# Cross attention and gated FFN on one core: the gate columns' load moved ahead, and the order of all engines up to the loop laid out anew

## The chip, the cores and the metric

The kernel runs on one core of a Trainium2 chip. A core has TensorE (matmuls; PE in the profile, its weight loads PEld), VectorE (DVE), ScalarE (ACT), GpSimd (POOL) and SyncE (SP), each of which works through its own instructions in order and waits on semaphores for the others, and 16 DMA engines that move data between HBM and the on-chip memory (SBUF). Matmul results go to PSUM, which has eight banks here. The metric is the device time in microseconds (us).

## The reference

Two stages. An attention between a sequence x (8 batches, 8 heads, 512 positions, 64 columns) and a small state (32 rows for each head), read in both directions with the same scores; its output is the input of a gated feed-forward network.

```
B, H, S, Ns, D = (8, 8, 512, 32, 64)
scores = scale * x @ state.T            # for each batch and head, scale = 1/8
xread  = softmax(scores) @ state        # 512 rows
sread  = softmax(scores.T) @ x          # 32 rows
t      = concatenate(xread, sread)      # 544 rows for each batch, 512 columns (8 heads of 64)
out    = (sigmoid(t @ w_gate) * (t @ w_val)) @ w_out      # 512 -> 1536 -> 512
```

Inputs and output are float32; the kernel computes its matmuls in bfloat16.

## The kernel before, in words

Since `xread` is a product with the small state, the kernel never forms it. It multiplies the state with the gate and value weights once for each batch (`sw_*`, giving SW: state rows by 1536 columns, for two groups of heads) and then multiplies SW with the transposed softmax weights aT (`gv_half`, `gv_mm`). So for each batch b there are these steps:

- `load_x`, `load_xh`, `load_xp` bring x; `cast_x`, `cast_xp` make it bfloat16. `xT_mm` transposes it on TensorE into PSUM and `xT_cp` copies that to SBUF (batches 0 and 1); from batch 2 on `at_xT_dma` transposes it with four DMAs on SP's queue, one for each quarter (chunk) c of the positions.
- `S_mm(b, i)` makes the scores: for batches 0 and 1 for half of the heads, from batch 2 on for chunks 2i and 2i + 1. `S_exp` takes the exponential, `n_sum` and `n_mul` sum and scale. `Sq_mm`, `Sq_exp`, `nq_sum`, `nq_mul` do the same for a quarter of the heads (one pair), batch 0 alone.
- The scaled weights are transposed to aT: `aT_mmc` and `aT_cp` (batches 0 and 1) or `aT_dma` (DMA transposes, later batches).
- `at_Eb`, `rd_mm` and `rd_fin` make `sread`: a bfloat16 copy of the exponentials on POOL, matmuls with x, and the division.
- `sw_half`, `sw_visit`, `sw_wide` make SW for a stretch of the weight columns; `sw_cp` copies a PSUM bank of it to SBUF, on ACT or DVE.
- `gv_half(b, f, w, place)` makes the gate (w = 0) or value (w = 1) of a block f of 128 of the 1536 columns; `gv_th` takes the tanh on ACT and `gv_glu` multiplies on DVE.
- `out_mm(b, k)` multiplies four blocks with w_out. From batch 1 on a Strassen-like scheme with sums (`t_sum`, `s_sum`) takes its place, in the loop.

The order of every engine is written out by hand: the kernel calls these helpers one after the other, and each engine gets its instructions in the order of the calls. Up to line 886 the calls are single lines (the stretch that the change lays out anew): the start, all of batch 0, the gates of batches 0 and 1, and the scores of batch 2. Then a loop (`step(b, f)`) runs over batches 2 to 8 and 12 blocks each, where batch 8 stands for the `sread` rows of all batches.

What sets the order beside the calls: each `place` is a set of PSUM banks that rotate (GV has two, SWP four, OU and AT one each), so a matmul into a bank waits for the copy out of its former content. DMAs with a cast, and some loads, are issued by POOL's queue: the weight columns (`load_w`), x of batches 0 to 3, w_out (`load_wo`, three thirds), the later state rows (`load_sb`). x of the later batches, the transposes and the stores of the output go by SP's queue. `warm` runs dummy matmuls into an unused bank.

The lines that the prediction's steps touch: L306 and L322 (SW matmuls), L385 and L373 (gate and value), L418 (`out_mm`), L154 and L163 (`S_mm`), L181 (`Sq_mm`), L285 (`rd_mm`), L147 (xT by DMA), L268 (aT by DMA), L103 and L85 (loads of x), L107 (weight columns), L114 (w_out), L551 (state rows), L593 (`pad`, which copies transposed state rows to a padded form on POOL), L233 (`n_mul`). L111 is `gate(landed)`: a copy of one column of a tile on POOL, so that POOL's queue holds until that tile has landed; in the old order it stands ahead of the load of batch 3's x and waits for batch 2's xT.

```
def gate(landed):
    nc.gpsimd.tensor_copy(pre[:, 1:2], landed)

def at_xT_dma(b):
    xT = xT_tile(b)
    for c in range(4):
        nc.sync.dma_start_transpose(xT[:, :, c], xbs[b][:, c].rearrange("p h d -> p (h d)"))
```

Of the kernel before, what the change touches and what calls it, by code (L numbers as in the profile page):

```python
# [16 lines left out]
def kernel(  # L17
# [86 lines left out]

    def load_w(w, lo, n):
        src = (moe_w_gate, moe_w_val)[w].rearrange("(k p) n -> p k n", p=128)
        nc.gpsimd.dma_start((wg, wv)[w][:, :, lo:lo + n], src[:, :, lo:lo + n])  # L107
# [533 lines left out]
    xT_mm(0, 1, GV)
    xT_cp(0, 0, vec)
    xT_cp(0, 1, vec)
    nq_sum(0, 3)
# [9 lines left out]
    xT_cp(1, 0, act, 2)
    xT_cp(1, 3, act)
    warm(2, AT)
    xT_mm(1, 2, GV)
    sw_half(0, 256, 256, 0, (OU, AT))
    nq_mul(0, 2, pool)
# [3 lines left out]
    sw_cp(0, 256, 0, 0, act)
    n_mulc(0, 0, 0, vec)
    S_mm(1, 0, SWP)
    aT_mmc(0, 1, SWP)
# [3 lines left out]
    aT_mmc(0, 0, SWP)  # L670
    at_Eb(0)
    aT_cp(0, 0, vec)
    aT_cp(0, 1, act)
    sw_half(0, 256, 256, 1, (GV, OU))
# [23 lines left out]
    sw_visit(1, 256, 256)
    gv_half(0, 9, 0, GV)
    sw_cp(0, 1024, 1, 0, vec)  # L700
    n_mul(1, 0, pool)
    sw_cp(1, 256, 2, 0, act)
    n_mul(1, 1, pool)
    sw_cp(0, 1024, 1, 1, vec)
    sw_cp(1, 256, 2, 1, act)
    load_w(0, 512, 512)
    aT_mmc(1, 1, AT)
    gv_glu(0, 3)
    at_Eb(1)
    aT_mmc(1, 0, GV)  # L710
    gv_th(0, 9)
    aT_cp(1, 0, vec)
    gv_half(0, 9, 1, OU)
    sw_visit(1, 1024, 256)
    load_sb(1)
    aT_cp(1, 1, act)
    sw_visit(0, 0, 256)
    sw_cp(0, 0, 2, 1, act)
# [24 lines left out]
    sw_cp(0, 1280, 2, 1, vec)
    load_w(1, 512, 512)
    load_x(2, nc.gpsimd)
    gv_half(0, 11, 0, GV)
    gv_th(0, 11)
    rd_fin(1)
    load_wo(0)
    sT_mm(1, SWP)  # L750
    gv_glu(1, 8)
    gv_half(0, 11, 1, AT)
    sT_cp(1, act)
    load_wo(1)
    gv_half(0, 1, 1, GV)
# [44 lines left out]
    gv_th(0, 7)  # L800
    gv_half(0, 7, 1, GV)
    sw_wide(2, 1)
    sw_cp(2, 1, 0, 1, act)
# [4 lines left out]
    out_mm(0, 0, AT)
    sw_cp(2, 1, 0, 0, vec)
    sw_visit(1, 0, 256)  # L810
    sw_cp(2, 1, 1, 0, act)
    sw_cp(2, 1, 2, 0, vec)
# [16 lines left out]
    gv_glu(1, 10)
    gv_glu(1, 6)  # L830
    out_mm(0, 4)
    out_mm(0, 11)
# [3 lines left out]
    gv_mm(1, 4, GV)
    gv_mm(1, 5, SWP)
    gv_glu(1, 1)
    t_sum(1, nc.vector)
    S_exp(2, 0)  # L840
    n_sum(2, 0)
    gv_th(1, 4)
    gv_th(1, 5)
    n_mul(2, 0, pool)
    S_mm(2, 1, AT)
    gv_glu(1, 5)
    S_exp(2, 1)
    n_sum(2, 1)
    out_mm(0, 1, GV)
    sw_wide(2, 0)  # L850
    sw_cp(2, 0, 1, 1, act)
    aT_dma(2, 0)
    n_mul(2, 1, pool)
    sw_cp(2, 0, 0, 0, act)
    at_Eb(2)
    sw_cp(2, 0, 2, 1, act)
    sw_cp(2, 0, 2, 0, vec)
    sw_cp(2, 0, 1, 0, act)
    out_mm(0, 3)
    aT_dma(2, 1)  # L860
    out_mm(0, 5)
    gv_mm(1, 7, SWP)
    gv_th(1, 7)
    gv_glu(1, 4)
    gv_mm(1, 11, GV)
    pad(4, 4)
    sw_cp(2, 0, 0, 1, vec)
    t_sum(2, nc.vector)
    t_sum(3, nc.vector)
    gv_th(1, 11)  # L870
    cast_x(3, pool, 4, 4)
    cast_x(3, act, 0, 4)
    gv_mm(1, 0, SWP)
    at_xT_dma(3)
    gv_th(1, 0)
    gv_glu(1, 11)
    out_mm(0, 6, GV)
    out_mm(0, 8)
# [202 lines left out]
```

## Time and profile before

| | before |
|---|---|
| device time, median of 3 runs | 213.7 us (213.7 to 214.9) |
| device time of the profiled execution | 214.2 us |
| its span, first to last instruction | 212.4 us |
| PE busy | 206.5 us, 97% |
| DVE busy | 162.0 us, 76% |
| ACT busy | 128.4 us, 60% |
| POOL busy | 73.0 us, 34% |
| granted clock of TensorE | 1.0 |
| moved by DMA | 27.01 MB |

The span leaves out what lies around the first and the last instruction. Matmuls are pipelined and their ends are modelled in the profile, so a busy PE is not PE at its peak, and an instruction's own duration is longer than the step from one matmul to the next. "Idle before" is the time that an engine waited ahead of an instruction, and the arrow names what ended it; a releaser is inferred from semaphores.

### The profile page before, as it was taken

What the parts mean: (1) busy time and instruction counts of PE and PEld (TensorE: products, weight loads), DVE (VectorE), ACT (ScalarE), POOL (GpSimd) and SP (SyncE); (2) the same over time, 40 slices, a digit from 0 to 9 for tenths busy, and PEclk for the clock granted to TensorE, in tenths of its full rate; (3) what the DMA queues carried; (4) which work ended last, traced back from release to release, by engine and by line L of the source; (5) the groups of instructions that cost most, each with busy time, mean ns of one, the idle gap of its engine ahead of it and who ended that gap; (6) DMA issues with size and microseconds to landing.
All of it is one profiled execution on the core that took longest, in us unless ns stands there. A gap on an engine that the chain in (4) does not pass through costs nothing.

```text
span 212.4 us, 5290 instructions
## 1 busy us (share of the span) xinstructions
PE 206.5 (97%) x2075; PEld 128.5 (60%) x2075; DVE 162.0 (76%) x315; ACT 128.4 (60%) x243; POOL 73.0 (34%) x101
## 2 busy tenths in 40 slices
PE   8899999999999999999999999999999999999992
PEld 2554433544565666565656575656666666788882
DVE  5698897784975779767986789588967787777882
ACT  3699696586778557865786478647874453233210
POOL 7899370259245404560437023902410000000000
PEclk9999999999999999999999999999999999999999
DMA  6999999685889544926911460245020400130026
GB/s 167 206 198 199 268 231 154 125 232 99 115 219 291 55 81 163 271 59 144 313 41 36 77 222 15 43 85 215 0 42 18 197 5 0 66 135 0 3 83 214
DMA packets 40152, 27.01 MB, mean 127 GB/s; under 512 B 23616, under 2 KB 37184, under 8 KB 40128
## 3 DMA queue, kind: packets, MB, share of 16 engines
q1 hardware_dynamic: 29376, 18.69, 33.8%
q0 software_dynamic: 10320, 7.67, 22.0%
q10 hardware_dynamic: 432, 0.33, 0.6%
q8 instruction: 16, 0.26, 0.5%
q14 instruction: 8, 0.07, 0.2%
HBM read 18.35 MB, written 8.91 MB: 128 GB/s over the span
## 4 chain that ended last, share of the span: by engine, by line
PE 86%; DMA 8%; ACT 2%; issue 1%; DVE 1%; SPq 0%; ACTq 0%
PE gvp L385 36%; PE outp L457 29%; DMA xf<-in_x_dram 8%; PE gvp L388 5%; PE swp L306 4%; PE outp L507 2%; PE outp L418 2%; PE swp L322 2%; PE gvp L373 1%; PE outp L476 1%; PE Sp L154 1%; PE rdp L282 1%; DVE glu L400 1%; ACT th L394 1%; PE Sp L163 0%
## 5 line engine op out<-in xcount | busy, mean ns | idle before, releaser
L394 ACT ACTIVATE th<-gvp 128x512 f32<-128x512 f32 (+1 forms) x108 | 62.1, 577 | 52.9 <-PE gvp L385 36.3
L385 PE MATMUL gvp<-aT,SW 128*128 128x512 bf16 x352 | 93.2, 379 | 0.1
L400 DVE SCALAR_TENSOR_TENSOR glu<-th,gvp 128x512 bf16<-128x512 f32 x96 | 65.1, 685 | 31.6 <-PE gvp L385 14.4
L359 ACT CAST SW<-swp 128x512 bf16<-128x512 f32 (+1 forms) x83 | 45.3, 581 | 8.0 <-PE swp L306 7.6
L385 PEld LDWEIGHTS <-SW 128*128 128x128 bf16 x352 | 32.2, 98 | 25.0 <-issue 6.2
L457 PEld LDWEIGHTS <-Sm 128*128 128x128 bf16 x324 | 31.7, 98 | 12.6
L206 POOL CAST Eb<-E 128x256 bf16<-128x256 f32 x32 | 17.5, 579 | 47.7 <-ACT E L174 47.7
L457 PE MATMUL outp<-tw,Sm 128*128 128x256 bf16 x240 | 31.8, 273 | 0.0
L457 PEld LDWEIGHTS <-glu 128*128 128x128 bf16 x240 | 23.5, 98 | 10.2
L457 PE MATMUL outp<-wo,glu 128*128 128x256 bf16 x168 | 22.9, 273 | 0.0
L233 POOL TENSOR_TENSOR ab<-E,ri 128x512 bf16<-128x512 f32 x14 | 14.6, 1050 | 19.4 <-DVE ri L216 19.2
L439 DVE TENSOR_TENSOR Sm<-glu 128x768 bf16<-128x768 bf16 (+1 forms) x27 | 15.3, 569 | 0.0
L465 DVE SCALAR_TENSOR_TENSOR res<-outp,U 128x512 f32<-128x512 f32 x19 | 13.0, 684 | 0.0
L388 PE MATMUL gvp<-XS,wgv 128*128 128x256 bf16 x96 | 12.6, 273 | 0.0
L174 ACT ACTIVATE E<-Sp 128x512 f32<-128x512 f32 x15 | 9.0, 603 | 4.9 <-PE Sp L154 3.8
L123 POOL CAST xb<-xf 128x1024 bf16<-128x1024 f32 x11 | 11.1, 1038 | 1.5 <-DMA xf<-in_x_dram 1.5
L406 DVE SCALAR_TENSOR_TENSOR glu<-th,gvp 128x128 bf16<-128x128 f32 x24 | 8.7, 462 | 3.8 <-PE gvp L388 3.7
L359 DVE CAST SW<-swp 128x512 bf16<-128x512 f32 (+1 forms) x17 | 10.1, 623 | 1.9 <-PE swp L322 1.7
L418 PE MATMUL outp<-wo,glu 128*128 128x512 bf16 x48 | 11.5, 379 | 0.0
L457 PE MATMUL outp<-wo,Sm 128*128 128x256 bf16 x84 | 11.5, 273 | 0.0
L214 DVE TENSOR_REDUCE rs<-E 128x16 f32<-128x512 f32 x15 | 10.2, 677 | 0.8 <-ACT E L174 0.8
L271 POOL CAST xs<-xf 128x1024 bf16<-128x1024 f32 x10 | 10.2, 1043 | 0.0
(105 smaller groups left out, 204.8 us busy)
## 6 DMA issues: line engine op xcount, KB each, us to landing
out_dram<-res SPq DMA_DIRECT2D x13, 512.0 KB, 2.9
xf<-in_x_dram SPq DMA_DIRECT2D x4, 1024.0 KB, 7.6
xf<-in_x_dram POOLq DMA_DIRECT2D x2, 1024.0 KB, 9.8
out_dram<-res SPq DMA_DIRECT2D x7, 256.0 KB, 3.0
wo<-in_moe_w_out_dram POOLq DMA_DIRECT2D x3, 512.0 KB, 10.6
wgv<-in_moe_w_gate_dram POOLq DMA_DIRECT2D x4, 256.0 KB, 7.6
wgv<-in_moe_w_val_dram POOLq DMA_DIRECT2D x4, 256.0 KB, 8.1
xf<-in_x_dram SPq DMA_DIRECT2D x3, 256.0 KB, 3.8
```

What stands on the lines that cost most here:

```text
L123: cp(xbs[b].rearrange("p c h d -> p h c d")[:, lo:lo + n], (xhs if b in xhs else xfs)[b][:, lo:lo + n])
L206: nc.gpsimd.tensor_copy(Ebs[b][:, c], E1s[b][:, c])
L233: (nc.gpsimd if eng is pool else nc.vector).tensor_tensor(half(b, i, abs_), e1, ri.unsqueeze(len(ri.shape)).to_broadcast(e1.shape), ALU.mult)
L359: cp(*sw_left.pop((b, lo, w, e)))
L385: nc.tensor.matmul(ps, SWs[b][:, g, w, fs], aTs[b][:, :, g], start=(g == 0), stop=(g == 1))
L388: nc.tensor.matmul(ps, (wg, wv)[w][:, j, fs], XS[:, :, j], start=(j == 0), stop=(j == 3))
L394: nc.scalar.activation(th, held["gv", b, f][0], AF.Tanh, scale=0.5)
L400: nc.vector.scalar_tensor_tensor(glus[b][:, f], held["th", b, f], 1.0, held["gv", b, f][1], ALU.add, ALU.mult)
L418: nc.tensor.matmul(ops[b, c], glus[b][:, f, c * 128:(c + 1) * 128], wo[:, f], start=(f == 0), stop=(f == NF - 1))
L439: nc.vector.tensor_tensor(Sm[:, t, i], a, c, op)
L457: nc.tensor.matmul(wps[key][:, c], lhs[:, i, c * 128:(c + 1) * 128], rhs[:, i], start=(first and c == 0 and i == 0), stop=(i == NF // 2 - ...
L465: nc.vector.scalar_tensor_tensor(to, wps[key], 0.5, held["w", name], ALU.mult, ALU.add)
```

## The change

The helper functions stay as they are; the list of calls up to the loop is another. The number of each kind of step is the same, but for the scores of batch 0: `S_mm(0, 0)`, `S_exp(0, 0)`, `n_sum(0, 0)` and two `n_mulc` (the first half of the heads) become two quarters with `Sq_mm`, `Sq_exp`, `nq_sum` and `nq_mul`. What the prediction speaks of:

- On POOL's queue `load_w(0, 256, 256)` (gate columns 256 to 511) stands ahead of the two loads of batch 1's x, where it stood behind them.
- The gate/value halves, SW groups, copies and GLUs of batches 0 and 1 stand in another order, with some copies on the other engine; `n_mul(1, 0)` moves from POOL to DVE, `sT_cp(1)` from ACT to DVE.
- `S_mm(2, 0)` stands behind `out_mm(0, 2)`, ahead of `gv_mm(1, 10)`, `gv_mm(1, 1)`, `out_mm(0, 4)`, `out_mm(0, 11)` and `sT_mm2`.
- POOL's queue: the load of w_out's last third between the two casts of batch 2's x; the load of batch 3's x behind the second cast, and `gate` behind `at_Eb(2)`; `pad(4, 4)` ahead of both `n_mul` of batch 2.

The core of the diff:

```diff
+    load_w(0, 256, 256)
     load_xh(1, 0, 4)
-    load_xh(1, 4, 4)
     make_identity(nc, ident)
     warm(2, OU)
-    load_w(0, 256, 256)
+    load_xh(1, 4, 4)
     load_w(1, 256, 256)
...
-    S_mm(0, 0, SWP)
...
-    S_exp(0, 0)
...
-    n_sum(0, 0)
-    n_mulc(0, 0, 1, vec)
...
+    Sq_mm(0, 0, GV)
...
+    Sq_mm(0, 1, SWP)
...
+    n_mul(1, 1, pool)
...
+    n_mul(1, 0, vec)
...
-    pad(2, 2)
...
-    cast_x(2, pool, 4, 4)
...
-    cast_x(2, pool, 0, 4)
-    at_xT_dma(2)
...
-    load_wo(2)
...
+    cast_x(2, pool, 0, 4)
+    load_wo(2)
...
+    cast_x(2, pool, 4, 4)
...
+    load_x(3, nc.gpsimd)
...
+    load_sb(2)
+    pad(2, 2)
...
+    at_xT_dma(2)
...
     out_mm(0, 9)
-    gv_mm(1, 10, SWP)
-    gv_th(1, 10)
-    out_mm(0, 2)
...
+    out_mm(0, 2)
+    S_mm(2, 0, SWP)
+    S_exp(2, 0)
+    out_mm(0, 11)
+    gv_mm(1, 10, GV)
...
-    gate(xTs[2][:, 0, 3, 0:1])
-    load_x(3, nc.gpsimd)
...
-    sT_mm2(SWP)
-    S_mm(2, 0, SWP)
-    sT_cp2(act)
...
+    sT_mm2(SWP)
+    S_mm(2, 1, OU)
...
+    pad(4, 4)
...
+    n_mul(2, 0, pool)
...
+    cast_x(3, pool, 4, 4)
...
+    at_Eb(2)
     gate(xTs[2][:, 0, 3, 0:1])
...
     at_xT_dma(3)
```

More of the change, by code (lines that the diff above doesn't have):

```diff
@@ L641 @@
[L641 to L644, printed above, removed]
+    xT_mm(0, 3, SWP)
+    warm(1, AT)
+    xT_mm(0, 0, GV)
+    sT_pad(1, act)
+    xT_cp(0, 3, vec)
+    Sq_mm(0, 3, SWP)
+    xT_cp(0, 0, act)
+    Sq_exp(0, 3)
+    xT_mm(0, 2, OU)
+    cast_xp(0, act, 2, 2)
+    Sq_mm(0, 0, GV)
+    xT_cp(0, 2, vec)
+    Sq_exp(0, 0)
+    warm(1, AT)
+    Sq_mm(0, 2, AT)
+    nq_sum(0, 3)
+    Sq_exp(0, 2)
+    xT_mm(0, 1, SWP)
+    xT_cp(0, 1, act)
+    warm(1, GV)
+    nq_sum(0, 0)
@@ L645 @@
+    sw_half(0, 256, 256, 0, (GV, OU))
+    warm(2, AT)
+    Sq_mm(0, 1, SWP)
+    xT_mm(1, 0, OU, 2)
     warm(2, AT)
-    S_mm(0, 0, SWP)
-    xT_mm(1, 0, GV, 2)
-    Sq_exp(0, 2)
-    nq_mul(0, 3, pool)
+    warm(1, AT)
+    sw_cp(0, 256, 0, 1, act)
     nq_sum(0, 2)
-    warm(1, AT)
-    xT_mm(1, 3, GV)
-    S_exp(0, 0)
[L654 to L659, printed above, removed]
-    n_sum(0, 0)
-    n_mulc(0, 0, 1, vec)
+    sw_cp(0, 256, 0, 0, act)
@@ L662 @@
+    Sq_exp(0, 1)
+    xT_cp(1, 0, act, 2)
+    nq_mul(0, 3, vec)
+    nq_mul(0, 0, pool)
+    nq_mul(0, 2, pool)
+    xT_mm(1, 2, SWP)
+    nq_sum(0, 1)
+    xT_mm(1, 3, GV)
+    S_mm(1, 0, OU)
+    nq_mul(0, 1, vec)
+    xT_cp(1, 3, vec)
+    aT_mmc(0, 1, SWP)
+    aT_mmc(0, 0, AT)
     xT_cp(1, 2, act)
[L663 to L666, printed above, removed]
     S_exp(1, 0)
+    at_Eb(0)
+    aT_cp(0, 1, act)
+    aT_cp(0, 0, vec)
     S_mm(1, 1, SWP)
-    sw_cp(0, 256, 0, 1, vec)
@@ L670 @@
[L670 to L674, printed above, removed]
+    load_sb(1)
+    load_w(0, 1280, 256)
     S_exp(1, 1)
-    rd_mm(0, GV)
+    sw_half(0, 256, 256, 1, (SWP, GV))
+    rd_mm(0, SWP)
+    n_sum(1, 0)
     sw_cp(0, 256, 1, 0, act)
-    gv_half(0, 3, 0, AT)
     sw_cp(0, 256, 1, 1, act)
-    gv_half(0, 2, 0, SWP)
-    n_sum(1, 0)
+    rd_fin(0)
+    gv_half(0, 2, 0, GV)
+    gv_half(0, 3, 0, OU)
+    gv_half(0, 2, 1, AT)
     sw_half(0, 1024, 256, 0, (SWP, SWP))
+    sw_visit(1, 256, 256)
@@ L698 @@
[L698 to L718, printed above, removed]
@@ L740 @@
-    gv_half(1, 3, 0, SWP)
-    gv_th(0, 1)
-    gv_th(1, 3)
[L743 to L755, printed above, removed]
-    pad(2, 2)
-    gv_half(0, 10, 0, GV)
+    sw_cp(0, 1024, 0, 1, act)
+    sw_cp(0, 1024, 1, 1, act)
+    n_mul(1, 0, vec)
+    gv_half(0, 8, 0, SWP)
+    sw_cp(0, 1024, 1, 0, vec)
@@ new lines @@
+    gv_glu(0, 2)
+    gv_glu(0, 3)
+    sw_cp(1, 256, 2, 1, vec)
+    gv_half(0, 9, 0, SWP)
+    aT_mmc(1, 1, SWP)
+    sw_cp(1, 256, 2, 0, act)
+    gv_th(0, 8)
+    aT_cp(1, 1, vec)
+    aT_mmc(1, 0, AT)
+    aT_cp(1, 0, vec)
+    gv_half(0, 9, 1, GV)
+    gv_th(0, 9)
+    gv_half(0, 8, 1, OU)
+    sw_visit(1, 1024, 256)
+    gv_glu(0, 9)
+    gv_glu(0, 8)
+    sw_visit(0, 0, 256)
+    load_w(0, 512, 512)
+    at_Eb(1)
+    sw_cp(1, 1024, 2, 0, act)
+    gv_half(1, 2, 0, GV)
+    rd_mm(1, AT)
@@ new lines @@
+    sw_cp(1, 1024, 2, 1, act)
+    gv_half(1, 8, 0, GV)
+    load_w(1, 512, 512)
+    gv_half(1, 2, 1, OU)
+    sw_cp(0, 0, 2, 0, vec)
+    gv_half(1, 8, 1, GV)
+    gv_th(1, 2)
+    sw_cp(0, 0, 2, 1, act)
+    gv_half(0, 1, 0, SWP)
+    gv_th(1, 8)
+    rd_fin(1)
+    sw_visit(0, 1280, 256)
+    gv_half(0, 1, 1, GV)
+    gv_half(1, 3, 0, SWP)
+    sT_mm(1, GV)
+    gv_half(0, 0, 0, SWP)
+    gv_glu(1, 2)
+    gv_glu(1, 8)
+    sw_cp(0, 1280, 2, 1, vec)
+    sw_cp(0, 1280, 2, 0, vec)
+    gv_half(0, 0, 1, SWP)
@@ L758 @@
+    load_x(2, nc.gpsimd)
+    load_sb(3)
+    gv_th(0, 1)
+    load_wo(0)
+    gv_half(0, 11, 0, AT)
+    sT_cp(1, vec)
+    load_wo(1)
+    gv_th(0, 0)
+    nc.scalar.activation(pre[:, 0:1], ones, AF.Exp)
+    gv_half(0, 11, 1, SWP)
+    gv_half(0, 10, 0, OU)
+    gv_half(1, 9, 0, GV)
+    gv_glu(0, 1)
+    cast_x(2, pool, 0, 4)
+    load_wo(2)
+    gv_half(1, 3, 1, GV)
+    gv_th(0, 11)
+    gv_glu(0, 0)
+    gv_th(1, 3)
+    gv_glu(0, 11)
+    gv_th(1, 9)
+    gv_th(0, 10)
     sw_visit(0, 512, 512, 0)
-    gv_glu(0, 0)
@@ L793 @@
-    gv_half(0, 7, 0, GV)
-    sw_cp(1, 512, 0, 0, act)
+    gv_half(0, 6, 1, GV)
+    gv_th(0, 4)
     gv_half(0, 5, 1, SWP)
+    gv_half(0, 7, 0, SWP)
+    load_x(3, nc.gpsimd)
     sw_cp(1, 512, 0, 1, act)
     sw_cp(1, 512, 1, 1, act)
+    sw_cp(1, 512, 1, 0, act)
+    sw_cp(1, 512, 0, 0, vec)
+    load_sb(2)
+    pad(2, 2)
+    gv_half(0, 7, 1, GV)
+    gv_glu(0, 4)
+    gv_th(0, 7)
+    sw_wide(2, 1)
+    gv_mm(1, 6, GV)
+    sw_cp(2, 1, 0, 0, act)
+    sw_cp(2, 1, 0, 1, act)
+    out_mm(0, 7, OU)
@@ L798 @@
+    out_mm(0, 0, AT)
     gv_glu(0, 6)
     gv_glu(0, 5)
[L800 to L803, printed above, removed]
+    at_xT_dma(2)
     gv_glu(0, 7)
-    gv_mm(1, 6, GV)
+    sw_cp(2, 1, 1, 0, vec)
+    sw_cp(2, 1, 2, 0, act)
     sw_cp(2, 1, 2, 1, act)
+    sw_visit(1, 0, 256)
+    sw_visit(1, 1280, 256)
     sw_cp(2, 1, 1, 1, act)
[L808 to L812, printed above, removed]
@@ L813 @@
-    sw_visit(1, 1280, 256)
-    out_mm(0, 7, OU)
-    gv_th(1, 6)
-    out_mm(0, 9)
-    sw_cp(1, 1280, 2, 0, act)
-    sw_cp(1, 1280, 2, 1, vec)
-    gv_mm(1, 10, SWP)
+    sw_cp(1, 0, 2, 0, act)
+    gv_th(1, 6)
+    sw_cp(1, 1280, 2, 1, act)
+    sw_cp(1, 1280, 2, 0, vec)
+    sw_cp(1, 0, 2, 1, vec)
+    t_sum(0, nc.vector)
+    gv_glu(1, 6)
+    out_mm(0, 9)
+    out_mm(0, 2)
[3 more added lines that the diff above has]
+    gv_mm(1, 10, GV)
+    n_sum(2, 0)
+    gv_mm(1, 4, SWP)
@@ L820 @@
     gv_th(1, 10)
-    out_mm(0, 2)
-    sw_cp(1, 0, 2, 1, vec)
-    sw_cp(1, 0, 2, 0, vec)
-    t_sum(0, nc.vector)
     gv_mm(1, 1, SWP)
+    gv_glu(1, 10)
+    t_sum(1, nc.vector)
+    gv_th(1, 4)
+    gv_mm(1, 5, GV)
     gv_th(1, 1)
-    gate(xTs[2][:, 0, 3, 0:1])
-    load_x(3, nc.gpsimd)
[L829 to L832, printed above, removed]
-    sT_mm2(SWP)
-    S_mm(2, 0, SWP)
-    sT_cp2(act)
[L836 to L873, printed above, removed]
+    sT_mm2(SWP)
+    S_mm(2, 1, OU)
+    t_sum(2, nc.vector)
+    gv_th(1, 5)
+    sT_cp2(act)
+    S_exp(2, 1)
+    pad(4, 4)
+    t_sum(3, nc.vector)
+    gv_glu(1, 1)
+    n_mul(2, 0, pool)
+    out_mm(0, 4)
+    out_mm(0, 1, GV)
+    out_mm(0, 3)
+    gv_glu(1, 5)
+    gv_glu(1, 4)
+    sw_wide(2, 0)
@@ new lines @@
+    aT_dma(2, 0)
+    n_sum(2, 1)
+    n_mul(2, 1, pool)
+    sw_cp(2, 0, 1, 0, act)
+    sw_cp(2, 0, 0, 1, act)
+    sw_cp(2, 0, 0, 0, act)
+    cast_x(3, pool, 4, 4)
+    out_mm(0, 5)
+    aT_dma(2, 1)
+    gv_mm(1, 7, SWP)
+    gv_mm(1, 11, GV)
+    gv_mm(1, 0, SWP)
+    out_mm(0, 6, GV)
+    sw_cp(2, 0, 2, 0, act)
+    gv_th(1, 11)
+    gv_th(1, 7)
+    out_mm(0, 8)
+    sw_cp(2, 0, 1, 1, vec)
+    cast_x(3, act, 0, 4)
+    gv_th(1, 0)
+    sw_cp(2, 0, 2, 1, vec)
+    at_Eb(2)
+    gate(xTs[2][:, 0, 3, 0:1])
@@ L874 @@
+    gv_glu(1, 11)
     at_xT_dma(3)
[L875 to L878, printed above, removed]
     out_mm(0, 10)
```

85 lines of the change are left out of this document (18 added, 67 removed).

## The prediction

> **What bounds the kernel now.** I read the page first, then busy time by stretches, then the chain of waits, then single engines around the places where the order changes.
>
> ```profile
> span 212.4 us, 5290 instructions
> ...
> PE 86%; DMA 8%; ACT 2%; issue 1%; DVE 1%; SPq 0%; ACTq 0%
> ```
> ```profile
> 4.50:13.40 8.90, 8.02 (x145) 5.32 (x145) 6.17 (x17) 6.38 (x13) 7.86 (x13) 1.00 1.41 207
> 13.40:32.05 18.65, 18.65 (x207) 7.71 (x204) 16.59 (x33) 15.69 (x33) 13.87 (x21) 1.00 1.31 228
> 32.05:41.78 9.73, 9.73 (x93) 4.40 (x93) 7.18 (x12) 5.56 (x11) 1.09 (x2) 1.00 1.09 139
> 41.78:54.65 12.87, 12.73 (x155) 5.84 (x151) 9.12 (x17) 9.47 (x19) 9.15 (x11) 1.00 0.65 164
> 54.65:185.00 130.35, 130.20 (x1263) 83.68 (x1257) 101.16 (x180) 83.22 (x154) 37.64 (x46) 1.00 0.43 108
> ```
>
> The columns after the length are busy us of PE, PEld, DVE, ACT and POOL, then the granted clock. From 13.40 on TensorE is busy in every stretch, at full clock, up to the tail. Its work is the same after the change: the same matmuls (eight of the 64-column score matmuls change their line) and 17 warm-up matmuls in both. So the end can move in three ways only: TensorE starts its dense work earlier than 13.4, an existing wait goes, or a new one comes. An edit that merely reorders work under a full TensorE is worth nothing.
>
> One wait stands where the profile's chain leaves TensorE, at the hand-over to the loop:
>
> ```profile
> 40.87 10.51 DMA xf<-in_x_dram
> ...
> 52.97 1.30 DVE glu L400 x2
> ...
> 54.31 0.41 PE swp L322 x7
> ```
> ```profile
> 44.94 0.63 PE L306 MATMUL swp<-wgv,sTc 64*32 64x512 bf16 x16
> ...
> 45.71 1.47 PE L418 MATMUL outp<-wo,glu 128*128 128x512 bf16 x6
> ```
> ```profile
> 53.35 0.63 PE L306 MATMUL swp<-wgv,sTc 64*32 64x512 bf16 x16
> ...
> 54.65 0.61 PE L385 MATMUL gvp<-aT,SW 128*128 128x512 bf16 x2
> ```
>
> The load of batch 3's x holds ACT's cast, the cast holds the tanh behind it, that holds the GLU on DVE, and the GLU holds the PSUM bank of the 24-matmul SW group. The undisturbed group occupies 45.71 - 44.94 = 0.77 us, this one 54.65 - 53.35 = 1.30 us: TensorE waits 0.53 us.
>
> **The change, part by part.** *The start.* The first gate columns trade places with batch 1's x, and batch 0's scores come in quarters, so its chain (exp, sum, scale, transpose) ends earlier.
>
> ```profile
> 5.00 0.78 POOL L107 DMA_DIRECT2D wgv<-in_moe_w_val_dram  x1
> ```
> ```profile
> wgv<-in_moe_w_val_dram POOLq DMA_DIRECT2D x1, 256.0 KB, 7.5
> ```
> ```profile
> 12.62 0.30 PE L306 MATMUL swp<-wgv,tw 64*32 64x256 bf16 x8
> ...
> 13.43 0.38 PE L385 MATMUL gvp<-aT,SW 128*128 128x512 bf16 x1
> ```
>
> The first value columns land at 5.00 + 7.5 = 12.5, and the SW half that needs them starts at 12.62. In the new order the same five transfers stand up to them on POOL's queue, so 12.5 stays; and this SW half and `rd_mm(0)` still stand ahead of the first gate matmul, so that cannot come before 12.5 + (13.43 - 12.62) = 13.3, against 13.43. The set of work done by then is the same. The gain is 0 to 0.1; I take 0. Against it, the second half of batch 1's x now lands one transfer later, and its transposes, copies and `S_mm(1, 1)` must pass before that SW half: up to 0.4 us lost. That would be hidden by the wait found below, which ends at a DMA and not at TensorE's own pace; alone it would cost its 0.4.
>
> *From 13.4 to 32.* Up to `sw_wide(2, 1)` the same set of gate/value halves and SW groups is permuted. ACT has 18.65 - 15.69 = 3.0 us free there and DVE 2.1. DVE takes over one `n_mul` and one `sT_cp` and gives two SW copies to ACT, roughly an exchange. POOL loses the `n_mul`, which brings forward only the issues behind it. I take 0, between a loss of 0.5 and none. No gain is possible, since TensorE shows no idle time there. The cover is the full TensorE; if a wait of a few tenths appears, it too shortens the wait below.
>
> *The scores of batch 2.* `S_mm(2, 0)` stands in the old order behind two `gv_mm`, three `out_mm` and `sT_mm2` counted from 37.00; in the new order only `out_mm(0, 2)` is left between.
>
> ```profile
> 37.00 1.03 PE L373 MATMUL gvp<-aT,SW 128*128 128x512 bf16 x4
> 37.87 1.03 PE L418 MATMUL outp<-wo,glu 128*128 128x512 bf16 x4
> ...
> 41.78 0.40 PE L154 MATMUL Sp<-sTz,xT 128*128 128x64 bf16 x8
> ```
>
> One such group lasts 37.87 - 37.00 = 0.87 us, so TensorE reaches `S_mm(2, 0)` at 37.00 + 0.87 = 37.87 and no more at 41.78. The scores read xT of batch 2, chunk 0 and, four matmuls on, chunk 1. These come by DMA transposes on SP's queue.
>
> ```profile
> 19.92 0.93 POOL L85 DMA_DIRECT2D xf<-in_x_dram  x1
> 20.81 1.53 POOL L114 DMA_DIRECT2D wo<-in_moe_w_out_dram  x2
> ...
> 29.20 2.02 POOL L123 CAST xb<-xf 128x1024 bf16<-128x1024 f32 x2 [1.19 <-DMA xf<-in_x_dram]
> 31.17 0.75 POOL L114 DMA_DIRECT2D wo<-in_moe_w_out_dram  x1
> 40.34 0.19 POOL L111 CAST pre<-xT 128x1 f32<-128x1 bf16 x1 [8.43 <-DMA xT<-xb]
> 40.87 0.91 POOL L85 DMA_DIRECT2D xf<-in_x_dram  x1 [0.34 <-PE outp L418]
> ```
> ```profile
> 31.25 6.38 SPq L147 DMA_TRANSPOSE xT<-xb  x4
> ...
> 45.45 7.33 SPq L268 DMA_TRANSPOSE aT<-ab  x4
> ```
> ```profile
> xf<-in_x_dram POOLq DMA_DIRECT2D x1, 1024.0 KB, 9.2
> ...
> wo<-in_moe_w_out_dram POOLq DMA_DIRECT2D x1, 512.0 KB, 12.4
> ...
> wo<-in_moe_w_out_dram POOLq DMA_DIRECT2D x1, 512.0 KB, 7.5
> ...
> xT<-xb SPq DMA_TRANSPOSE x1, 7.7
> ...
> xT<-xb SPq DMA_TRANSPOSE x1, 6.7
> ...
> xf<-in_x_dram POOLq DMA_DIRECT2D x1, 1024.0 KB, 10.5
> ...
> aT<-ab SPq DMA_TRANSPOSE x1, 6.1
> ```
> ```profile
> L147 SPq DMA_TRANSPOSE xT<-xb x4: 1217/1260/1273, 72.5 to 76.3; - x4
> ...
> DMA to landing us min/median/max: 2.5/2.5/2.5
> ```
>
> The numbers at the ends are us from issue to landing, each of one DMA: the load of batch 2's x (issued 19.92), the second and third third of w_out (the second issued half of 1.53 behind 20.81, the third at 31.17), the first two transposes of xT (31.25, and one issue of 1.3 later, 32.6), batch 3's x (40.87), the first transpose of aT (45.45). On free DMA engines, in the loop, a transpose lands 2.5 after its issue. Beside a load it takes 6 to 8, and it ends just behind that load: w_out's third lands at 31.17 + 7.5 = 38.7, the transposes at 31.25 + 7.7 = 38.95 and 32.6 + 6.7 = 39.3; batch 3's x lands at 40.87 + 10.5 = 51.4, the transpose of aT at 45.45 + 6.1 = 51.55. Old TensorE arrived at 41.78, after 39.3, and never saw this; the old gate at 40.34 kept batch 3's x out of these transposes' way.
>
> The change puts both together. On POOL the third load of w_out now stands between the two casts: casts at 29.2 and 30.95, transposes issued from 31.95 on, 0.7 later than before. Right behind the second cast, at 31.95 as well, POOL issues batch 3's x; the gate, moved behind `at_Eb(2)`, holds nothing any more. So a load of a megabyte is in flight beside the transposes, behind w_out's third.
>
> When does it land? Batch 2's x lands at 29.1 and w_out's second third at 21.6 + 12.4 = 34.0: 2.4 us each for two loads with as many bytes to read as batch 3's x. At that pace w_out's third lands at 36.4 and batch 3's x at 38.8: the lower end. The upper end is its own 10.5 from issue, 42.4. The nearest row is w_out's third, which beside the transposes and two small state loads took 38.7 - 34.0 = 4.7 and not 2.4, so I take a value in the upper half, 41.0. Chunk 1 landed 39.3 - 38.7 = 0.6 behind its load: 41.6, between 39.4 and 43.0. TensorE is ready at 37.87 and stands still for 3.7 us (1.5 to 5.1). Every engine's queue goes on behind that, and TensorE has no slack later to win it back.
>
> [...]
>
> *The hand-over.* Batch 3's x lands some 10 us before its casts are due, so the 0.53 us at 54.31 goes: next late there is the aT of batch 2. Its scaling on POOL now stands behind `pad(4, 4)`, a new wait for the state transposes (`sT_mm2`, ACT's copies); behind it queue both `n_mul`, the cast of batch 3 and Eb.
>
> ```profile
> 44.38 1.04 POOL L233 TENSOR_TENSOR ab<-E,ri 128x512 bf16<-128x512 f32 x1 [2.61 <-DVE ri L216]
> ...
> 49.87 1.28 POOL L593 COPY sTz<-sTc 64x512 bf16<-64x512 bf16 x2
> ```
>
> With `S_mm(2, 0)` ending at 41.9, five groups of 0.87 and `sT_mm2` (as long as half a group) bring 46.7, copies a similar half 47.2, the pad 48.5, two `n_mul` of 1.04 50.6; four transposes 1.3 apart with one store between leave SP by 54.5 and land 2.5 later, 57.0. The loop needs them at 54.65 + 3.2 = 57.85. The margin of 0.8 is thin but enough: cost 0.
>
> **The sum.** 3.7 - 0.5 = +3.2 us, from +1.0 (1.5 - 0.5) to +4.6. The profiled execution took 214.2 (span 212.4 and 1.8 around it) and would take 217.4; it lies 0.5 above the median of the runs, 213.7, so the forecast is 213.7 + 3.2 = **216.9**.
>
> **Rivals.** *Held back no more than before* (0.24): the transposes suffer from w_out's third alone. Chunk 1 lands at the old 39.3, or 6.7 after its new issue at 33.3, 40.0: wait 1.4 to 2.1, time 214.6 to 215.3. For it: batch 3's x queues behind w_out's third. Against it: aT ended behind batch 3's x itself.
>
> *The transposes get their turns* (0.10): chunk 1 lands 2.5 after 33.3, at 35.8, before 37.87. Then nothing waits, the 0.53 is won, and the time is 213.2, not slower. It decides at one point: chunk 1 landed by 37.87. For it stands the loop's 2.5; against it three transposes in the rows above. [...]
>
> *Faster by over 1%* (0.04): TensorE would have to be dense 2 us before 13.4, against the value columns' 12.5; so perhaps the columns land earlier than their place says.
>
> *The aT of batch 2 comes late as well* (0.07): one of its transposes behind stores takes 6.1 instead of 2.5, landing at 60.6, 2.8 past its due time: 219.7.
>
> **How the numbers follow.** The main case has 0.55 and covers 215.6 to 218.4. Over 1% is 2.1 us, beyond 215.8 or below 211.6; the three runs shown spread over 0.6%, so less would hardly be told from none. Slower: 0.55 less a sliver of 0.02 near its lower end, plus 0.07, 0.60. Within 1%: 0.24 + 0.10 + 0.02 = 0.36. Faster: 0.04. The range 213.0 to 218.7 holds nearly all of the main case and the first two rivals and leaves out some 0.17.
>
> **What would show it.** In the new profile: first gate matmul at 13.3 to 13.8; POOL's issue of batch 3's x near 32; TensorE idle for 2 to 5 us from about 38 before the scores of L154, with the DMA of xT as releaser; chunk 1 landing just behind batch 3's x; the SW group at the loop's head back at 0.77 us. I am wrong if L154 starts near 38 with no idle time before it, or if TensorE has its idle time somewhere before 32.

## The result and the profile after

The changed kernel takes 223.2 us (median of 5 runs, 222.1 to 223.9) against 213.7 for the kernel before: 1.043 times its time, 95% interval 1.039 to 1.047. The direction was forecast; the size, 9.5 us, is three times the 3.2 forecast and lies outside the range.

The head of the profile after and its chain by engine:

```profile
span 221.3 us, 5286 instructions
...
PE 78%; DMA 13%; POOL 3%; ACT 2%; issue 1%; SPq 1%; DVE 0%; POOLq 0%; ACTq 0%
```

TensorE holds 78% of the chain where it held 86%, and DMA 13% where it held 8%. The view by stretches (length, busy us of PE, PEld, DVE, ACT and POOL, granted clock, DMA share, GB/s) says where:

```profile
4.50:13.49 8.99, 7.89 (x147) 5.14 (x147) 5.92 (x16) 7.76 (x17) 8.54 (x14) 1.00 1.40 205
13.49:32.60 19.11, 18.52 (x206) 7.76 (x202) 16.18 (x33) 15.07 (x33) 10.57 (x16) 1.00 1.33 227
32.60:38.73 6.13, 6.08 (x60) 2.35 (x60) 3.55 (x7) 4.38 (x9) 2.69 (x5) 1.00 1.18 158
38.73:48.80 10.07, 3.37 (x16) 1.41 (x16) 2.17 (x4) 1.19 (x2) 0.00 (x0) 0.66 0.99 131
48.80:63.50 14.70, 14.60 (x165) 6.84 (x166) 9.83 (x17) 9.92 (x19) 7.76 (x12) 1.00 0.28 82
```

The start is as long as before (13.49 against 13.43). One stretch of ten microseconds, 38.73 to 48.80, has TensorE busy for 3.37 of them at two thirds of its clock. The first gate matmul of the loop comes at 63.50 and not at 54.65: 8.85 later, which is the whole difference of the two spans (8.9). TensorE in order of time there:

```profile
36.99 1.90 PE L418 MATMUL outp<-wo,glu 128*128 128x512 bf16 x8
44.87 0.39 PE L154 MATMUL Sp<-sTz,xT 128*128 128x64 bf16 x4 [5.98 <-DMA xT<-xb]
45.98 0.40 PE L154 MATMUL Sp<-sTz,xT 128*128 128x64 bf16 x4 [0.72 <-DMA xT<-xb]
46.19 1.90 PE L418 MATMUL outp<-wo,glu 128*128 128x512 bf16 x4
```

Eight output matmuls at one per 0.215 us end at 38.71; then TensorE stands until chunk 0 of xT(2) has landed, runs four score matmuls, and stands again for chunk 1. POOL's row of issues, and what each DMA took from issue to landing:

```profile
31.12 0.75 POOL L114 DMA_DIRECT2D wo<-in_moe_w_out_dram  x1
31.86 1.05 POOL L123 CAST xb<-xf 128x1024 bf16<-128x1024 f32 x1
32.85 0.91 POOL L85 DMA_DIRECT2D xf<-in_x_dram  x1
33.74 0.75 POOL L551 DMA_DIRECT2D Sm<-in_state_dram  x1
```
```profile
32.95 8.84 SPq L147 DMA_TRANSPOSE xT<-xb  x4
```
```profile
wo<-in_moe_w_out_dram POOLq DMA_DIRECT2D x1, 512.0 KB, 7.2
...
xf<-in_x_dram POOLq DMA_DIRECT2D x1, 1024.0 KB, 11.9
...
xT<-xb SPq DMA_TRANSPOSE x1, 11.9
...
Sm<-in_state_dram POOLq DMA_DIRECT2D x1, 64.0 KB, 12.2
...
xT<-xb SPq DMA_TRANSPOSE x1, 11.5
```

Batch 3's x lands at 32.85 + 11.9 = 44.75 and the first transpose at 32.95 + 11.9 = 44.85; the state rows land at 33.74 + 12.2 = 45.9 and the second transpose, issued at 34.4, at 45.9 too. The first four matmuls aside (0.2 us at this clock, 46.19 - 45.98 for the second four), TensorE stood for 6.2 + 0.9 = 7.1 us, where 3.7 were forecast.

The clock was not forecast at all. The same view cut at the granted clock:

```profile
38.73:41.97 3.24, 0.16 (x1) 0.00 (x0) 1.23 (x2) 0.00 (x0) 0.00 (x0) 1.00 1.03 233
41.97:44.87 2.90, 0.00 (x1) 0.01 (x1) 0.00 (x0) 0.00 (x0) 0.00 (x0) 0.50 1.70 115
44.87:48.80 3.93, 3.21 (x15) 1.40 (x16) 0.94 (x2) 1.19 (x2) 0.00 (x0) 0.50 0.45 60
```

The clock fell to half 3.3 us after the work ran out and stayed there for 3.93 us after it came back. The 2.8 us from 45.98 on, at half speed, cost 1.4.

The hand-over to the loop is as forecast, 63.50 - 62.73 = 0.77 us for the SW group:

```profile
62.73 0.62 PE L306 MATMUL swp<-wgv,sTc 64*32 64x512 bf16 x16
63.17 0.40 PE L322 MATMUL swp<-wgv,sTc 64*32 64x512 bf16 x8
63.50 1.04 PE L385 MATMUL gvp<-aT,SW 128*128 128x512 bf16 x4
```

So the two profiled executions add up: TensorE came to the scores at 38.71 instead of 37.87 (0.84 late), stood for 7.1, lost 1.4 to the clock and won 0.53 back: 8.8 of the 8.85.

### The profile page after: what moved, and what is told of

Its sections match the earlier page's. It is cut to its first block, busy times and chain, and to the rows that moved or that the text cites. A ratio compares the mean times of both kernels' runs of the same rounds, so it can differ in the third digit from the quotient of the medians.

```text
span 221.3 us, 5286 instructions
## 1 busy us (share of the span) xinstructions
PE 207.9 (94%) x2072; PEld 128.6 (58%) x2075; DVE 160.3 (72%) x313; ACT 130.3 (59%) x249; POOL 70.7 (32%) x100
## 4 chain that ended last, share of the span: by engine, by line
PE 78%; DMA 13%; POOL 3%; ACT 2%; issue 1%; SPq 1%; DVE 0%; POOLq 0%; ACTq 0%
PE gvp L385 28%; PE outp L457 28%; DMA xf<-in_x_dram 8%; DMA xT<-xb 5%; PE gvp L388 5%; PE outp L418 4%; PE gvp L373 3%; PE swp L306 3%; PE outp L507 2%; PE Sp L154 1%; PE outp L476 1%; PE swp L322 1%; POOL wgv L107 1%; PE rdp L282 1%; ACT th L394 1%
## 5 line engine op out<-in xcount | busy, mean ns | idle before, releaser
L359 ACT CAST SW<-swp 128x512 bf16<-128x512 f32 (+1 forms) x88 | 47.5, 578 | 11.1 <-PE swp L306 8.9
L206 POOL CAST Eb<-E 128x256 bf16<-128x256 f32 x32 | 16.0, 530 | 49.8 <-ACT E L174 49.8
L233 POOL TENSOR_TENSOR ab<-E,ri 128x512 bf16<-128x512 f32 x13 | 13.9, 1066 | 17.4 <-DVE ri L216 16.3
L174 ACT ACTIVATE E<-Sp 128x512 f32<-128x512 f32 x14 | 8.4, 602 | 12.2 <-PE Sp L154 11.7
L214 DVE TENSOR_REDUCE rs<-E 128x16 f32<-128x512 f32 x14 | 9.5, 680 | 7.1 <-ACT E L174 7.1
L418 PE MATMUL outp<-wo,glu 128*128 128x512 bf16 x45 | 11.9, 402 | 0.2
L457 PE MATMUL outp<-wo,Sm 128*128 128x256 bf16 x84 | 11.5, 273 | 0.0
L154 PE MATMUL Sp<-sTz,xT 128*128 128x64 bf16 x96 | 5.2, 197 | 6.7 <-DMA xT<-xb 6.7
L359 DVE CAST SW<-swp 128x512 bf16<-128x512 f32 (+1 forms) x12 | 7.7, 664 | 4.5 <-PE swp L322 2.6
```

The costliest lines, as they stand in the source:

```text
L206: nc.gpsimd.tensor_copy(Ebs[b][:, c], E1s[b][:, c])
L233: (nc.gpsimd if eng is pool else nc.vector).tensor_tensor(half(b, i, abs_), e1, ri.unsqueeze(len(ri.shape)).to_broadcast(e1.shape), ALU.mult)
L359: cp(*sw_left.pop((b, lo, w, e)))
L418: nc.tensor.matmul(ops[b, c], glus[b][:, f, c * 128:(c + 1) * 128], wo[:, f], start=(f == 0), stop=(f == NF - 1))
L457: nc.tensor.matmul(wps[key][:, c], lhs[:, i, c * 128:(c + 1) * 128], rhs[:, i], start=(first and c == 0 and i == 0), stop=(i == NF // 2 - ...
```

## The experiments

All ratios are to the kernel before, measured beside each run on the same chip. The first four change one thing each in the changed kernel.

**Batch 3's x back behind the transposes.**

```diff
-    load_x(3, nc.gpsimd)
     sw_cp(1, 512, 0, 1, act)
...
     gv_th(1, 6)
+    gate(xTs[2][:, 0, 3, 0:1])
+    load_x(3, nc.gpsimd)
...
     at_Eb(2)
-    gate(xTs[2][:, 0, 3, 0:1])
```

> The changed kernel with one thing undone: POOL again reads a column of chunk 3 of xT(2) before it issues batch 3's x, so that load no longer shares the DMA engines with the four transposes. Theory A (x of batch 3 in front holds the transposes): they land behind w_out's third (38.3), chunk 1 between 39 and 41; TensorE, ready at 38.7, waits 0.5 to 2.3 us instead of 7.1; no half clock; batch 3's x lands near 51 and the SW group at the loop's head costs 0.5 more again. Time 216.4 (214.8 to 217.6). Theory B (the state rows in 128-byte packets hold them): they still land after 43 and the time stays over 219. Theory C (TensorE is late for other reasons and the wait only shows it): no gain over 1 us, 222 to 223.5.

215.0 us, ratio 1.006 (1.004 to 1.008). TensorE in order of time:

```profile
38.52 0.29 PE L154 MATMUL Sp<-sTz,xT 128*128 128x64 bf16 x4 [0.55 <-DMA xT<-xb]
38.98 0.29 PE L154 MATMUL Sp<-sTz,xT 128*128 128x64 bf16 x4 [0.18 <-DMA xT<-xb]
```

The two waits are about 0.7 and 0.35 us, counted by the matmul stream as above (the brackets count from the modelled end of the matmul before), instead of 7.1; the clock stays full, and 8.2 of the 9.5 us are gone. Theories B and C fall. The half microsecond at the loop's head that A expected back did not come: x landed at 47.9, not near 51.

**The state rows out of the way.** `load_sb(2)` moved up, behind `load_sb(3)`.

> The changed kernel with the state rows of batches 4 and 5 loaded some 13 us earlier, right behind those of 6 and 7, so that no 128-byte packets run beside batch 3's x and the transposes. Theory A (batch 3's x alone holds chunk 0): x still lands at 43.5 to 45 and chunk 0 with it; only the second wait of 0.9 us (chunk 1 behind the state rows) may go. Time 222.2 (221.3 to 223.4). Theory B (the small packets slow everything on that queue): x lands by 42, the wait falls to under 4 us, time 218 to 220.

222.4 us, ratio 1.040 (1.038 to 1.043). Chunk 0 still lands with x, at 44.3; only the wait for chunk 1 is gone, as theory A had it. The median is 0.7 us lower than that of the changed kernel, but the intervals of the two ratios overlap, so that gain is seen in the trace and not shown in the time.

**The scores back behind `sT_mm2`, x still early.** Their exp and sum move with them.

```diff
-    S_mm(2, 0, SWP)
-    S_exp(2, 0)
     out_mm(0, 11)
...
     sT_mm2(SWP)
+    S_mm(2, 0, SWP)
```

> The changed kernel with the first scores of batch 2, their exp and their sum put back behind sT_mm2, as the kernel before has them; batch 3's x stays early. Theory A (the time is lost because TensorE stands at the scores): four and a half groups of work (4.8 us) fill the wait; TensorE reaches the scores at 43.4 and waits 1.4 + 0.9; it is idle for less than 3 us, so the clock is not halved. Time 217.0 (216.0 to 218.5). Theory B (the landing of the transposes sets the end through the chain scores, n_mul, aT, whatever TensorE does meanwhile): 220 to 222.

219.3 us, ratio 1.027 (1.022 to 1.031), between the theories, because the wait moved to a place that neither had named:

```profile
45.86 1.03 PE L575 MATMUL stp<-ident,Sm 128*128 128x64 bf16 x16 [2.58 <-DMA Sm<-in_state_dram]
```

`sT_mm2` needs the state rows that stand behind x in POOL's queue. And the clock fell here too, though TensorE stood for only 2.6 us; the 3 us of the expectation, an estimate beside the changed kernel's 3.3, did not hold:

```profile
42.04:43.12 1.08, 1.08 (x6) 0.39 (x4) 1.08 (x2) 0.81 (x2) 0.00 (x0) 1.00 1.00 130
43.12:45.46 2.34, 0.16 (x1) 0.00 (x0) 0.10 (x1) 0.37 (x1) 0.00 (x0) 1.00 1.44 129
45.46:48.88 3.42, 2.80 (x35) 2.20 (x37) 0.69 (x1) 1.64 (x4) 1.20 (x2) 0.50 0.38 103
```

**Work for TensorE in the gap.** `warm(24, SWP)` ahead of `S_mm(2, 0, SWP)`.

> The changed kernel with 24 matmuls on constants (5.2 us at full clock) put on TensorE right ahead of the first scores of batch 2; they read nothing that is loaded and nobody reads them. Theory A (the half clock from 42.0 to 48.8 is what TensorE's idle time brings): the scores start as late as without them, 44.9, but at full clock; time 1.4 us less, 221.8 (221.0 to 222.5). Theory B (the half clock has another cause, or it costs nothing because the transposes set the pace): 222.7 to 223.7, with half clock still there or without gain.

```profile
37.56 5.34 PE L541 MATMUL warm<-wm 128*128 128x512 bf16 x24
44.12 0.29 PE L154 MATMUL Sp<-sTz,xT 128*128 128x64 bf16 x4 [1.21 <-DMA xT<-xb]
45.12 0.29 PE L154 MATMUL Sp<-sTz,xT 128*128 128x64 bf16 x4 [0.71 <-DMA xT<-xb]
...
61.27 1.04 PE L385 MATMUL gvp<-aT,SW 128*128 128x512 bf16 x4
```

In the profiled execution the clock stays full. From the second four scores to the loop it is 61.27 - 45.12 = 16.15 us, against 63.50 - 45.98 = 17.52: the half clock cost 1.4. The median, 222.3 (220.8 to 224.1), shows less of it: ratio 1.038 (1.031 to 1.044), overlapping that of the changed kernel. The executions above 223 have a mean clock of 0.99 instead of 0.997, so there the clock fell for a while all the same; they have no trace that says why. That idle time halves the clock, and the 1.4, rest on the traces; a gain in the median is not shown.

The next two change the load.

**Batch 3's x as bfloat16,** half the bytes written (`load_xh(3, 0, 8)` in its place; the copy for `rd_mm` reads it too).

> The changed kernel with batch 3's x loaded as bf16 (converted on the way, half the bytes written, the same bytes read), at the same place on POOL; the casts read the bf16 copy. Theory A (the load and the transposes slow each other while both have bytes under way; the size of the load sets how long): x lands some 2 to 3 us earlier, 41.5 to 43, chunk 0 with it, TensorE waits 3 to 4.5 instead of 6.1; time 219.0 to 221.5. Theory B (only the order counts: bytes read, not written): lands at 44 to 45, no gain, 222 to 223.5.

221.0 us, ratio 1.031 (1.027 to 1.036): theory A in the time and in x's landing, 41.7. Chunk 0 did not land with x, though, but 2.0 ahead of it; chunk 1 came 0.9 behind it:

```profile
39.76 0.29 PE L154 MATMUL Sp<-sTz,xT 128*128 128x64 bf16 x4 [1.76 <-DMA xT<-xb]
42.57 0.40 PE L154 MATMUL Sp<-sTz,xT 128*128 128x64 bf16 x4 [2.53 <-DMA xT<-xb]
```

**The early load alone, in the kernel before.** `load_x(3, nc.gpsimd)` behind the second cast (so ahead of w_out's third), `gate` removed.

> The kernel before with one thing of the change alone: batch 3's x is issued right behind the second cast of batch 2, and POOL's wait for chunk 3 of xT(2) is gone; every other order is the old one. Theory A (this load alone holds the transposes): chunk 0 lands with x, near 44 to 45 instead of 38.9; TensorE, at the scores at 41.8, waits 3 to 4 us, with little or no half clock; the loop's head gains 0.5. Time 216.5 (215.3 to 218.0). Theory B (the transposes are late in the changed kernel through its other orders): chunk 1 lands by 41.8, no wait, 213.2 to 214.

218.6 us, ratio 1.020 (1.017 to 1.023); neither theory had it. The issues to landing, of x (issued 31.28), the first transpose (31.36), w_out's third (32.17) and the second transpose (32.70):

```profile
xf<-in_x_dram POOLq DMA_DIRECT2D x1, 1024.0 KB, 8.7
...
xT<-xb SPq DMA_TRANSPOSE x1, 8.6
...
wo<-in_moe_w_out_dram POOLq DMA_DIRECT2D x1, 512.0 KB, 11.1
...
xT<-xb SPq DMA_TRANSPOSE x1, 10.6
```
```profile
43.36 1.89 PE L418 MATMUL outp<-wo,glu 128*128 128x512 bf16 x8 [3.51 <-DMA wo<-in_moe_w_out_dram]
```

Chunk 0 lands at 31.36 + 8.6 = 39.96 with x (31.28 + 8.7 = 39.98), chunk 1 at 43.3 with w_out's third (32.17 + 11.1 = 43.3). Each transpose ends with the load issued just ahead of it. Here the late DMA that TensorE met first was w_out's third itself, 3.5 us for an output ahead of the scores. This profiled execution is the shortest of its four, 217.5 us at full clock; the others took 218.4 to 218.8 at a mean clock of 0.992, so about a microsecond of the loss is not in this trace.

Two runs put the mechanism to the question.

**x issued behind the transposes, but long before they land.** POOL first reads an element that ACT writes near 34.

```diff
-    load_x(3, nc.gpsimd)
     sw_cp(1, 512, 0, 1, act)
...
+    gate(SWs[2][:, 1, 1, 1280:1281])
+    load_x(3, nc.gpsimd)
     sw_visit(1, 0, 256)
```

> The changed kernel with batch 3's x issued near 35.5 instead of 32.9, behind the issue of two or three of the four transposes but long before they land: POOL first reads an element that ACT writes then. Theory A (a transpose is reported landed only behind what was issued ahead of it): chunks 0 and 1 land with w_out's third, 38.5 to 39.5, only chunks 2 and 3 behind x at 44 to 47; TensorE waits for 0.5 to 1.5 us at the first scores, and perhaps again at the second; time 215 to 217.5. Theory B (any load under way slows every transpose under way): chunks 0 and 1 land after 41, time 219 to 222.5.

215.0 us, ratio 1.006 (1.005 to 1.008): theory A in its numbers. The landings of the transpose issued at 32.08, of the one at 33.8, of x (34.89), and of the last two (35.2 and 36.6):

```profile
xT<-xb SPq DMA_TRANSPOSE x1, 6.9
...
xT<-xb SPq DMA_TRANSPOSE x1, 5.4
...
xf<-in_x_dram POOLq DMA_DIRECT2D x1, 1024.0 KB, 8.5
...
xT<-xb SPq DMA_TRANSPOSE x2, 8.1
```

The two issued ahead of x land at 39.0 and 39.2, just behind the state rows (38.8); the two issued behind it at 43.8 and 44.3, just after x at 43.4. Between the second and the third, 1.4 us at the issue became 4.6 at the landing. The mere issue of x, then, held neither of the two transposes that were under way (39.0 and 39.2 against 43.4). But in the trace no packet of 2 KB or more moves from 35.0 to 38.2, where those of x have some 3,600 bytes (see the end), while SP's queue moved 0.24 MB, nearly all of two chunks (0.26 MB). So x had hardly begun to move when these two were through, and the run does not tell "behind what was issued ahead" from "slowed by the load whose bytes move meanwhile".

**No transpose beside a load at all.** x right behind w_out's third, and POOL holds the second cast until x has landed (the state rows early as above).

```diff
     load_wo(2)
+    load_x(3, nc.gpsimd)
...
+    gate(xfs[3][:, 7, 3, 0:1])
     cast_x(2, pool, 4, 4)
```

> The changed kernel with batch 3's x issued right behind w_out's third, and the second cast of batch 2 held on POOL until that x has landed, so that no transpose runs beside a load; the state rows are loaded early. Theory A (load and transposes slow each other): w_out's third lands by 37.5 and x 2.5 to 3.5 later, 39.5 to 41, not 44.3; the transposes, issued from 41 to 42, land 2.5 each behind their issue, chunk 1 near 45; TensorE waits as long as in the changed kernel and the time is 221.5 to 223.5. Theory B (the load is slow by itself): x lands at 43 to 45, the transposes end near 49, the time is 225.5 to 227.5.

223.4 us, ratio 1.047 (1.045 to 1.049): theory A, near the edge of its numbers (w_out's third came at 38.2, 0.7 later than it allowed). Landings of w_out's third (issued 30.42), x (31.16) and the four transposes (from 42.32, 1.3 apart):

```profile
wo<-in_moe_w_out_dram POOLq DMA_DIRECT2D x1, 512.0 KB, 7.8
...
xf<-in_x_dram POOLq DMA_DIRECT2D x1, 1024.0 KB, 9.9
...
xT<-xb SPq DMA_TRANSPOSE x4, 2.5
```

x lands at 41.1, 2.9 behind w_out's third; in the changed kernel it was 44.75 - 38.3 = 6.4 behind. Each transpose then takes 2.5, and the scores start at 44.87 once more. Issuing the first transposes nine microseconds sooner, beside the loads, had brought nothing for chunk 0 and 0.2 us for chunk 1.

The last four ask what else the change costs or wins.

**x and the scores both back.** The edits of the first and the third run together.

> The changed kernel with both taken back: batch 3's x behind chunk 3 of xT(2), and the first scores of batch 2 behind sT_mm2. What is left of the change is the new start, the quarters of batch 0 and the other orders up to 32 us. Theory A (the whole loss lies in those two): the 1.06 us that TensorE still waited at the scores with the load put back goes too; 213.9 (213.3 to 214.6). Theory B (the start has a price of its own, w_gate's and w_val's last columns a microsecond later): 214.5 to 215.5.

215.5 us, ratio 1.007 (1.005 to 1.009). The 1.06 us at the scores are gone, but `sw_wide(2, 0)` now waits for a PSUM bank:

```profile
47.67 0.41 PE L322 MATMUL swp<-wgv,sTc 64*32 64x512 bf16 x7 [0.82 <-DVE glu L400]
```

The time is at the upper end of theory B's, but this wait comes from the order of the edit and not from the start, so the run says nothing of the start.

**x back, the state rows early, the scores behind two more groups.**

> The changed kernel with batch 3's x behind chunk 3 of xT(2), the state rows of batches 4 and 5 loaded early, and the first scores of batch 2 behind two more groups of TensorE (a third of an output, a gate group; 1.7 us). Theory A (with x3 put back only the 1.06 us at the scores were lost; the new start costs nothing): no wait at the scores, none taken over elsewhere; 213.7 (213.1 to 214.3). Theory B (a wait of about a microsecond turns up later whatever the order, or the start costs it): 214.6 to 215.6.

214.9 us, ratio 1.007 (1.005 to 1.009). The time is theory B's. Again there is no wait for xT, but there are two for GV's banks, 0.4 us each by the matmul stream, both released by a GLU. Whether the start costs anything is still open.

**x back, the scores behind `out_mm(0, 11)` alone.**

```diff
     out_mm(0, 2)
+    out_mm(0, 11)
     S_mm(2, 0, SWP)
     S_exp(2, 0)
-    out_mm(0, 11)
```

> The changed kernel with batch 3's x behind chunk 3 of xT(2) and the first scores of batch 2 behind one more group of TensorE, a third of an output (0.87 us) for which everything is there; nothing else differs from the run in which only the load was put back (1.006 of the time before, TensorE 1.06 us at the scores). Theory A (those 1.06 us are all that was left of the loss, so the new start and the orders up to 32 us cost nothing): 0.8 us of them go, 1.002 of the time before (1.000 to 1.004). Theory B (the rest lies elsewhere, in the start): 1.005 to 1.007, with TensorE waiting elsewhere or reaching the scores later.

214.0 us, ratio 1.001 (0.999 to 1.003). TensorE finds its scores nearly ready, and the loop's first gate comes at 54.39:

```profile
38.72 0.67 PE L154 MATMUL Sp<-sTz,xT 128*128 128x64 bf16 x8
...
54.39 1.04 PE L385 MATMUL gvp<-aT,SW 128*128 128x512 bf16 x4
```

That is theory A. With two calls put right, the changed kernel is as fast as the one before: what is left of the change (the start, the quarters, the orders up to 32 us and the hand-over), taken together, costs no more than 0.6 us and wins no more than 0.2, by the interval. No version beat the kernel before.

**The hand-over's half microsecond, in the kernel before.** `load_x(3, nc.gpsimd)` becomes `load_xh(3, 0, 8)` there.

> The kernel before with batch 3's x loaded as bf16, at its old place. Theory A (in the kernel before, this load and the transposes of aT(2) beside it make batch 3's hand-over 0.5 us late): x lands 2 to 4 us earlier, the SW group at the loop's head falls from 1.30 to 0.77 us, 213.2 (212.8 to 213.6). Theory B (the hand-over is late for another reason): no difference, 213.5 to 214.0.

213.8 us, ratio 1.000 (0.998 to 1.002): the time is theory B's, though the wait is gone from its profile, where the group that began at 53.47 ends at 54.24, after 0.77 us, as theory A had it:

```profile
53.47 0.63 PE L306 MATMUL swp<-wgv,sTc 64*32 64x512 bf16 x16
...
54.24 1.04 PE L385 MATMUL gvp<-aT,SW 128*128 128x512 bf16 x4
```

The profiled execution of the kernel before took 214.2 and the median 213.7. The likeliest reading is that the 0.53 us were most of that difference, a wait which the median execution does not have; those executions have no trace, so this is argued and not shown.

## Why the prediction was right in kind and wrong in size

- *The start: 0.* Right. 13.49 in the profile, and the run with two calls put right is at 1.001.
- *13.4 to 32: 0, loss up to 0.5.* Right in the median, by the same run. In the profiled execution of the changed kernel TensorE waited 0.58 us at 27.18 for the last value columns and batch 2's x landed a microsecond later than before; the other traces with the same start show waits of 0.3 or less up to 32 us. "It too shortens the wait below" was wrong: that delay moves the casts, and so x and the transposes, by as much.
- *The mechanism.* Right. TensorE meets the scores early, and the transposes end behind a load that the gate used to hold back: putting the load back takes 8.2 of 9.5 us away, and the early load alone makes the kernel before 2% slower.
- *"When does it land?"* This step failed: 41.0 taken, 44.75 measured. Up to 0.9 of the miss is the later issue (32.85, not 31.95); the rest is the pace, for in the three runs that issued x at 31.7 to 32.1 and left its size alone it landed at 43.9 to 44.4. 41.0 is what x does with no transpose beside it (41.1 in the run that held the casts). Beside them it needed 3.5 us more, counted from w_out's third. The row for that stood in my own paragraph: w_out's third beside the transposes took 4.7 us and not 2.4. I used it to lean toward the upper half of a range instead of as the pace of both loads, which gives 34.0 + 4.7 + 4.7 = 43.4 and, with twice as many bytes to write, later (with half of its bytes, as bfloat16, x came at 41.7). The upper end was wrong as well: x's own 10.5 from issue came from a stretch with less in front of it; it took 11.9. (The sum's lower end, 213.7 + 1.0 = 214.7, and the 215.6 at which the main case begins don't agree either; both are far from 223.)
- *"0.6 behind its load."* Chunk 0 was 0.1 behind x; chunk 1 came with the state rows, another load issued in between, 1.1 behind x. I had counted only x in its way.
- *The omitted term.* The wait of 7.1 us cost 1.4 more at half clock. The forecast wait of 3.7 could have cost some of it too, since the clock fell 3.3 us after the work ran out.
- *The hand-over: 0.53 won.* Seen in the trace, and by the last run most likely not in the median. Without it, 0.84 + 7.1 + 1.4 = 9.3 stands against the 9.5 between the medians.
- *aT late as well.* Did not happen; the loop's head shows no wait.
- *Held back no more than before* and *the transposes get their turns* fell: chunk 1 landed 11.5 us behind its issue. For the second: SP's queue did move a packet for each of POOL's (608 and 609, shown at the end), but a transpose's packets are small and many, some 240 bytes and 544 to a chunk.

## What to carry to other kernels

Price a DMA by what is issued ahead of it on every queue, not by its own length: here a small transpose issued behind a megabyte load ended with that load (44.85 and 44.75, 39.96 and 39.98), except where the load was converted on its way (39.7 and 41.7). Where two transfers will run side by side, use the row in which they did. Before work is moved ahead on the busiest engine, check when its operand lands, and if a wait of several microseconds threatens, count the slower clock behind it (here 1.4 us behind a wait of 7.1).

## What the runs showed of the hardware

**Landing order across queues.** A transpose on SP's queue landed with or just behind the loads that POOL had issued ahead of it (39.96 and 39.98, 43.3 and 43.3, 44.85 and 44.75), and ahead of one issued after it (39.2 and 43.4). These landings are no strict rule of issue order: with x as bfloat16, the first transpose, issued 0.1 us behind x, landed at 39.7 and x at 41.7. What ties a transpose's landing to that of a load, the runs do not show.

**Packets of the two queues.** The bytes of the transposes came late, too. The packets, MB and share of the 16 engines that POOL's queue (q0) and SP's (q1) moved in the changed kernel from 38.30 to 44.30, ahead of the two landings:

```profile
q0 software_dynamic: 609, 0.94, 79.2%
q1 hardware_dynamic: 608, 0.15, 52.7%
```

One packet each, and nearly so in every microsecond from 39 to 44 (65 and 63 in the first, 52 and 48 in the last). But a packet of the transposes has some 240 bytes (SP's queue moved 2,176 for the four, 0.52 MB, from 32.95 to 48, so 544 for a chunk of 128 KB), and one of x some 3,600 (0.52 MB in 144 between 39 and 41). So the transposes moved as many packets as POOL's loads and still only 0.15 MB against 0.94. It is not the whole account: by 44.30 SP's queue had moved some 900 packets, and chunk 0 had not landed.

The load pays too: from the issue of x to its landing all queues together moved 166 GB/s in the changed kernel (32.85 to 44.75) and 217 in the run that held the casts (31.16 to 41.06), the rest of w_out's third among them. Why the two together move less than the load alone is open.

**The clock.** It was at half for 6.83 us in the changed kernel (41.97 to 48.80) and for 3.42, half as long, with the scores late (45.46 to 48.88). The fall at 41.97 came 3.3 us after the work ran out (38.71), the one at 45.46 only 2.3 (43.12), within a wait of 2.6. So the length of the idle time does not decide alone: with the early load in the kernel before, a wait of 3.5 us (up to 43.36) left the clock full in the profiled execution. What else decides, the runs do not show.
